# Attention block on one core: the second addition of each VectorE row, the weighted copies of V and the normalising products move to POOL

## The chip, the cores and the metric

The kernel runs on one core of a Trainium2 chip. The metric is the device time of one execution in microseconds, and times of several runs are given as their median. A core has five engines that run side by side, each through its own queue in a fixed order: PE (TensorE, matrix products), ACT (ScalarE), DVE (VectorE), POOL (GpSimd) and SP (SyncE, here only DMAs). They wait for one another through semaphores. An instruction that waits holds up everything behind it on its engine.

## The reference

```python
B, S, D = x.shape            # 1, 2048, 448
H = 16; Dh = D // H          # 28
qkv = (x @ wqkv).reshape(B, S, 3, H, Dh).transpose(2, 0, 3, 1, 4)
q, k, v = qkv[0], qkv[1], qkv[2]
scores = einsum("bhqd,bhkd->bhqk", q, k) * (Dh ** -0.5)
p = softmax(scores, axis=-1)
o = einsum("bhqk,bhkd->bhqd", p, v)
return o.transpose(0, 2, 1, 3).reshape(B, S, D) @ wo
```

All tensors are bf16. It is a whole attention block without a mask: three projections, 16 heads of width 28 over 2048 positions, and an output projection.

## The kernel before, in words

The work is cut into 16 units: four groups of four heads, g, times four chunks of 512 queries, c. Unit u has 16 steps over the keys, 128 keys each. One step of one unit is called a row here, and 256 rows are numbered r = 16u + kt. A row is four tiles, one for each head of the group: 128 keys by 512 queries of scores. So there are 1024 tiles.

PE writes the scores of a tile into one bank of PSUM (s_mm, line 904). The exponential is then made in one of two ways.

- Most tiles go to ACT. It reads three or two banks at once (banks 0 to 2 and 3 to 4 in turn) and writes bf16 exponentials into PT (line 966). PE then multiplies PT with V in one pass of four products (line 871).
- The rows in PLAN["rows"], 67 of them before, go to DVE. It reads each of the four tiles from one of the three other banks (pool "M") and writes the sum of score and constant, cut off below, as int16 into DY (line 928, called D1 here). These bits, read as fp16, are a rough exponential. To make it finer, two shifted copies of the whole row, DS0 and DS1, are made from DY by adding a constant to 128x2048 int16 values (line 936). PE makes three passes for such a row: DY with V, and DS0 and DS1 with two weighted copies of V, called VW (line 859; 32 of them over the kernel, 128x512 each). DY and DS have three buffers each (NDR, NDS), so at most three rows of this kind are under way.

A bank of pool "M" is also held through each unit by the sums that the passes build up, and the rest serve D1's tiles, the projections, the output projection and zero products that PE runs as filling (line 484).

After a unit DVE copies the sums to OTS (line 723). For units 0 to 13 four DMAs on SP's queue (L1 to L4, with a reciprocal on DVE at line 733) bring the reciprocals of the row sums, spread over partitions, into RB, and DVE multiplies RB with OTS (line 739, called NM). Units 14 and 15 do this through PE (norm_pe, last_unit). With the last group of heads the output projection follows (line 710), its result is copied to OUTS by DVE (line 698) and stored by a DMA (line 700). For the last unit ACT makes two of the four copies (line 696), and ACT's own queue issues their DMAs.

The order on every engine is not written by hand. Each instruction is put down with P.add, with its dependencies, a duration in ns and a priority, and schedule() (line 125) lays the instructions out on a timetable made of these durations; each engine then runs its list in that order. The durations are thus part of the order and no more than that: on the chip only dependencies and the order count. CFG holds weights of this planner, PLAN the rows for DVE and the due times of later projections. CFG["dlead"] says how many tiles ahead of its own place a DVE row may start (line 978), and nslack how long after the planned landing of its DMA the NM is placed.

Of the kernel before, what the change touches and what calls it, by code (L numbers as in the profile page):

```python
# [7 lines left out]
ALU = mybir.AluOpType  # L8
# [55 lines left out]
class _Prog:  # L64
# [272 lines left out]
PHASE = (0, 344, 682)  # L337
# [3 lines left out]
ZLO = -ZADD  # L341


CFG = {"late": 4.5, "load": 1.5, "load0": 18, "dcost": 2.3, "dlead": 30.385592406, "aslack": 235.147215477, "opp": 0.0, "oload": 2.5, "klead": 0.405674492, "vlag": 0.024622608, "hot1": 45000.0, "hotm": 3600.0, "nslack": 2585.717981114, "dlook": 20.0, "plook": 471.074451806, "rcost": 4.9, "rlead": 1.0, "rend": 4, "rgap": 2, "acost": 0.4455, "dprio": 0.651412491, "nride": 4, "rslack": 300.0, "stail": 24, "jprio": -0.750113813, "sdlap": 4.771128299, "vwlead": 1.249363626, "sdpen": 6.528606395, "rcostx": -0.000676632}

PLAN = {
    "rows": [9, 14, 16, 24, 26, 28, 33, 38, 41, 50, 53, 54, 57, 61, 62, 70, 72, 77, 80, 84, 88, 95, 97, 98, 103, 107, 109, 111, 113, 117, 123, 125, 131, 135, 138, 139, 141, 148, 149, 152, 162, 163, 164, 165, 169, 176, 177, 179, 180, 187, 189, 190, 193, 199, 200, 207, 211, 212, 213, 215, 222, 229, 231, 234, 235, 244, 248],
    "late": [1.281070854, 1.964014751, 1.915657661, 0.76, 2.743900482, 1.159356603, 1.904466413, 1.845975994, 2.106524837, 2.189415295, 2.428349574, 2.873971098, 2.728623137, 3.84085501, 2.733578841, 4.131340808, 3.508351422, 5.446684044, 4.832243098, 4.46548081, 5.163206443, 7.002171665, 6.90767575, 7.804407036, 4.947925744, 6.78739139, 5.302922841, 6.89552453, 9.777227448, 10.389677342, 7.735503962, 7.490566717, 8.23514301, 7.360578973, 7.83742904, 10.319692841, 8.329224918, 8.680463746],
}


def _fast(nc, x, wqkv, wo, out, n_heads=16):
# [9 lines left out]
    NK = NST  # L362
    QCH = 512
    NCH = S // QCH
    NQT = QCH // 128
# [3 lines left out]
    NDR = 3  # L369
    NDS = 3  # L370
    NPH = len(PHASE)
    NMENG = "dve"
    NOB = 4
    scale = float(DH) ** -0.5
    VONE = DH
# [5 lines left out]
    of = out.rearrange("b s d -> (b s) d")  # L381
# [4 lines left out]
    P = _Prog()  # L386
    es = ExitStack()
    with es:
# [66 lines left out]
        def dma_of(t, g):  # L455
# [3 lines left out]
                      dur=300, prio=-12, name="iota")  # L459
        id_f_op = P.add("dve", lambda e: e.tensor_scalar(id_f[:, :], iota_i[:, :], 0.0, None, ALU.is_equal),  # L460
                        deps=[io_op], dur=250, prio=-10, name="id_f")
# [6 lines left out]
        def zero_pass(acc_open, t):  # L468
# [12 lines left out]
            def emit(e):  # L481
                ins = None
                for h in range(4):
# [13 lines left out]
                       deps=[id_f_op], dur=100, prio=-6, name="sel")  # L497
# [194 lines left out]
        def out_tile(n, opm, hold, eng, pr):  # L692
            oi = outs_n[0] % NOB
            outs_n[0] += 1
            if eng == "act":
                fe = (lambda e: e.activation(OUTS[:, oi, :], bank(hold.banks[0])[:, 0:D], AF.Identity))  # L696
            else:
                fe = (lambda e: e.tensor_copy(OUTS[:, oi, :], bank(hold.banks[0])[:, 0:D]))  # L698
            opev = P.add(eng, fe, deps=[opm, outs_last[oi]], dur=550, prio=pr, name=f"OPEV{n}", rel=[(hold, 0)])
            outs_last[oi] = P.add("act" if eng == "act" else "sp", (lambda e: e.dma_start(of[n * 128:(n + 1) * 128, :], OUTS[:, oi, :])),  # L700
                                  deps=[opev], after=[outs_last[oi]], dur=60, prio=pr, name=f"ODMA{n}", dma_group=grp_out[oi],
                                  nbytes=128 * D * 2)

# [15 lines left out]
        def post_unit(u, last_pv):  # L719
            g, c = units[u]  # L720
            ub = u % 2
            pr = u + 1.02
            accev = P.add("dve", (lambda e: e.tensor_copy(OTS[:, ub, :], bank(pv_open[u].banks[0]))),  # L723
                          deps=[last_pv, ots_last[ub]], dur=610, prio=pr - 60.0, name=f"ACCEV{u}", rel=[(pv_open[u], 0)])
            us = slice(u * 16, (u + 1) * 16)
            if u == NU - 2:
                norm_pe(u, accev, pr)
                return
            l1 = P.add("sp", (lambda e: e.dma_start(scr_l[u], OTS[VONE:128:32, ub, :])), deps=[accev], dur=100, prio=pr,
                       name=f"L1_{u}", dma_group=grp_l[0], nbytes=8192)  # L730
# [8 lines left out]
            nm = P.add(NMENG, (lambda e: e.tensor_tensor(OTN[:, g, c * QCH:(c + 1) * QCH], RB[:, ub, :], OTS[:, ub, :], ALU.mult)),  # L739
                       deps=[l4] + list(xt_ev.values()), dur=1200 if NMENG == "pool" else 610, prio=pr + 0.2, name=f"NM{u}", slack=CFG["nslack"])  # L740
            ots_last[ub] = nm
            finish_unit(g, c, nm, pr)

# [98 lines left out]
        def pv(u, kt):  # L842
# [13 lines left out]

            if r in n_row and (g, kt // 4) not in vw_ev:
                c4 = kt // 4
                vw_ev[(g, c4)] = [P.add("dve", (lambda e, k=k: e.tensor_scalar(VW[:, g % 2, k, 4 * c4:4 * c4 + 4, :], V[:, 4 * c4:4 * c4 + 4, g * 128:(g + 1) * 128],
                                                                              WTERM[k + 1], None, ALU.mult)),  # L860
                                        deps=[v_ev[(g, c4)], vw_used.get((g % 2, c4))], dur=200, prio=u + kt / NK - CFG["vwlead"], name=f"VW{k}_{g}_{c4}")
                                  for k in range(NPH - 1)]

            def weights(k, h):
# [46 lines left out]
        def row_tile(r, h, partner, p_pr):  # L911
            u, kt = r // NK, r % NK
            g, c = units[u]
            t = (u, kt, h)
            if r not in n_row:
                n_row[r] = len(n_row)
                row_ops[r] = []
            ri = n_row[r] % NDR
            old = row_pv.get((n_row[r] - NDR, 0))
            prev_row = row_at.get(n_row[r] - NDR, [])  # L920
            assert n_row[r] < NDR or old is not None, "DVE rows too close"
            deps = [kq_ev[(0, g, c)], kq_ev[(1, g, kt // 4)]]
# [5 lines left out]
            o1 = P.add("dve", (lambda e, ri=ri, h=h, s=s: e.tensor_scalar(DY[:, ri, h * 512:(h + 1) * 512], bank(s.banks[0]), ZLO, ZADD, ALU.max, ALU.add)),  # L928
                       deps=[s, old] + prev_row, dur=600, prio=-90.0, name=f"D1_{r}_{h}", rel=[(s, 0)])
# [6 lines left out]
            row_ev[r] = [P.add("dve", (lambda e, k=k: e.tensor_scalar(DS[:, k, rk, :], DY[:, ri, :], float(PHASE[k + 1]), None, ALU.add)),  # L936
                               deps=row_ops[r] + [row_pv.get((n_row[r] - NDS, k + 1))], dur=600, prio=pr + 0.001 * k, name=f"DS{k}_{r}") for k in range(NPH - 1)]
            row_at[n_row[r]] = row_ev[r]
            done.update(4 * r + j for j in range(4))

# [811 lines left out]
```

## Time and profile before

| | |
|---|---|
| median of 3 runs | 362.06 us (362.02 to 362.64) |
| the profiled execution | 362.26 us |
| its span, first to last instruction | 360.4 us |
| PE, ACT, DVE, POOL busy | 342.2, 345.5, 321.8, 3.4 us |
| granted TensorE clock | 1.000 |
| DMA traffic | 9.91 MB |

Busy time is the union of an engine's instructions; where instructions overlap in the records, the sum of their durations is larger. PE's products are pipelined and partly run beside one another, so that a busy PE isn't a PE at its peak. The view of instruction groups gives source line, engine, operation, output and input with shape, the count, then the busy time in us and the mean of one in ns, and then the idle time of the engine just before these instructions and what ended it. The timeline gives start and length in us.

### The profile page before, as it was taken

How to read it: one execution, taken by the hardware profiler on the slowest of the kernel's cores; microseconds unless marked ns; L12 is line 12 of the kernel's file. 1: busy time of each engine (PE TensorE's matmuls, PEld its weight loads, DVE VectorE, ACT ScalarE, POOL GpSimd, SP SyncE). 2: the span in 40 equal slices, each digit the busy share in tenths (PEclk: the TensorE clock that was granted, in tenths of full speed). 3: DMA queues.
4: the chain of work that ended last, by engine and by line, in shares of the span. 5: the costliest groups of instructions: out<-in, count | busy, mean ns of one | idle time of the engine just before them, and what ended most of it. 6: DMA issues, size and time to landing. Idle time of an engine off the chain costs nothing.

```text
span 360.4 us, 8848 instructions
## 1 busy us (share of the span) xinstructions
PE 342.2 (95%) x3885; PEld 114.4 (32%) x3885; DVE 321.8 (89%) x574; ACT 345.5 (96%) x307; POOL 3.4 (1%) x9
## 2 busy tenths in 40 slices
PE   8999999999999999999999999999998989999996
PEld 4444322332223243223333323332222222234323
DVE  6579999798999999999999998999999999999504
ACT  2999999999999999999999999999999999999992
POOL 3000000000000000000000000000000000000000
PEclk9999999999999999999999999999999999999999
DMA  8600000100100000000000000000000001010201
GB/s 232 152 2 3 2 32 5 32 2 3 33 0 5 32 18 17 2 32 3 20 15 5 31 2 32 3 14 22 29 4 3 20 15 32 16 44 28 78 29 54
DMA packets 13940, 9.91 MB, mean 27 GB/s; under 512 B 7504, under 2 KB 12048, under 8 KB 13896
## 3 DMA queue, kind: packets, MB, share of 16 engines
q1 hardware_dynamic: 13096, 8.74, 8.4%
q8 instruction: 31, 0.51, 0.6%
q10 hardware_dynamic: 800, 0.56, 0.5%
q14 instruction: 13, 0.11, 0.1%
HBM read 7.23 MB, written 2.06 MB: 26 GB/s over the span
## 4 chain that ended last, share of the span: by engine, by line
ACT 88%; PE 11%; issue 0%; ACTq 0%; DVE 0%
ACT PT L966 87%; PE ps L904 3%; PE ps L871 2%; PE ps L555 2%; PE ps L484 1%; PE ps L789 1%; PE ps L572 0%; PE ps L538 0%; ACT OUTS L696 0%; PE ps L824 0%; PE ps L758 0%; PE ps L809 0%; PE ps L769 0%; PE ps L710 0%; ACT QT L524 0%
## 5 line engine op out<-in xcount | busy, mean ns | idle before, releaser
L966 ACT ACTIVATE PT<-ps 128x1536 bf16<-128x1536 f32 (+1 forms) x303 | 342.5, 1398 | 1.0 <-PE ps L904 0.9
L928 DVE TENSOR_SCALAR DY<-ps 128x512 int16<-128x512 f32 x268 | 175.4, 685 | 9.3 <-PE ps L904 8.1
L904 PE MATMUL ps<-QT,KT 28*128 28x512 bf16 x1024 | 151.6, 384 | 12.9 <-ACT PT L966 8.4
L936 DVE TENSOR_SCALAR DS<-DY 128x2048 int16<-128x2048 int16 x134 | 89.9, 683 | 0.4
L904 PEld LDWEIGHTS ps<-QT,KT 28*128 28x128 bf16 x1024 | 39.7, 91 | 139.0 <-ACT PT L966 101.5
L871 PE MATMUL ps<-PT,V 128*32 128x512 bf16 x756 | 65.8, 385 | 0.7 <-DVE OTS L723 0.4
L871 PE MATMUL ps<-DS,VW 128*32 128x512 f16 x536 | 49.3, 385 | 0.1
L555 PE MATMUL ps<-xT,w_raw 112*32 112x512 bf16 x512 | 35.8, 381 | 0.0
L484 PE MATMUL ps<-ZM,ZW 128*32 128x512 bf16 x324 | 29.5, 410 | 1.2 <-DVE ZM L466 1.2
L871 PE MATMUL ps<-DY,V 128*32 128x512 f16 x268 | 26.5, 385 | 0.1
L871 PEld LDWEIGHTS ps<-PT,V 128*32 128x32 bf16 x756 | 17.1, 94 | 28.4 <-issue 21.9
L871 PEld LDWEIGHTS ps<-DS,VW 128*32 128x32 bf16 x536 | 12.5, 94 | 20.5 <-issue 13.7
L572 PE MATMUL ps<-w_raw,xT 112*128 112x112 bf16 x256 | 17.1, 214 | 0.0
L555 PEld LDWEIGHTS ps<-xT,w_raw 112*32 112x32 bf16 x512 | 12.2, 95 | 13.1 <-issue 3.8
L698 DVE CAST OUTS<-ps 128x448 bf16<-128x448 f32 x14 | 8.6, 622 | 7.6 <-PE ps L710 7.2
L572 PEld LDWEIGHTS ps<-w_raw,xT 112*128 112x128 bf16 x256 | 13.0, 98 | 6.7 <-issue 4.7
L528 DVE CAST KT<-ps 128x512 bf16<-128x512 f32 x16 | 11.0, 689 | 3.5 <-PE ps L555 3.4
L484 PEld LDWEIGHTS ps<-ZM,ZW 128*32 128x32 bf16 x324 | 7.8, 99 | 13.6 <-issue 10.9
L528 DVE CAST V<-ps 128x448 bf16<-128x448 f32 x16 | 9.9, 621 | 2.0 <-PE ps L572 1.9
L526 DVE TENSOR_SCALAR QT<-ps 128x512 bf16<-128x512 f32 x15 | 10.3, 686 | 1.5 <-PE ps L555 1.5
L710 PE MATMUL ps<-wop,XO 128*128 128x448 bf16 x48 | 11.5, 355 | 0.0
L723 DVE COPY OTS<-ps 128x512 f32<-128x512 f32 x15 | 10.3, 687 | 0.5 <-PE ps L871 0.5
(49 smaller groups left out, 79.2 us busy)
## 6 DMA issues: line engine op xcount, KB each, us to landing
RB<-scr_r SPq DMA_DIRECT2D x14, 256.0 KB
out_dram<-OUTS SPq DMA_DIRECT2D x14, 112.0 KB, 1.7
XO<-in_x_dram SPq DMA_DIRECT2D x3, 448.0 KB, 6.3
w_raw<-in_wqkv_dram SPq DMA_DIRECT2D x5, 196.0 KB, 6.3
wop<-in_wo_dram SPq DMA_DIRECT2D x16, 24.5 KB
XO<-in_x_dram SPq DMA_DIRECT2D x1, 224.0 KB, 3.5
XO<-in_x_dram ACTq DMA_DIRECT2D x1, 224.0 KB, 4.0
scr_l<-OTS SPq DMA_DIRECT2D x14, 8.0 KB
```

Source lines behind the costliest of these rows:

```text
L484: ins = e.matmul(ps[32 * h:32 * h + 32, b * 512:(b + 1) * 512], ZW[:, :], ZM[:, :], start=shut, stop=shut, skip_group_check=not shut, tile ...
L526: fe = (lambda e: e.tensor_scalar(evac[0](), evac[1](hold[0].banks[0]), mul, None, ALU.mult))
L528: fe = (lambda e: e.tensor_copy(evac[0](), evac[1](hold[0].banks[0])))
L555: ins = e.matmul(ps[32 * h:32 * h + 32, b * 512:(b + 1) * 512], w_raw[0:IT, it, col:col + 32], xT[0:IT, it, c * 512:(c + 1) * 512], start= ...
L572: ins = e.matmul(ps[:, b * 512 + j * GD:b * 512 + (j + 1) * GD], xT[0:IT, it, n * 128:(n + 1) * 128], w_raw[0:IT, it, 2 * D + g * GD:2 * D ...
L710: return e.matmul(bank(hold[0].banks[0])[:, 0:D], OTN[:, gg, n * 128:(n + 1) * 128], wop[:, gg, :], start=(gg == 0), stop=(gg == G - 1))
L723: accev = P.add("dve", (lambda e: e.tensor_copy(OTS[:, ub, :], bank(pv_open[u].banks[0]))), deps=[last_pv, ots_last[ub]], dur=610, prio=pr ...
L871: ins = e.matmul(ps[32 * h:32 * h + 32, b * 512:(b + 1) * 512], weights(k, h), p_[h], start=(kt == 0 and k == 0), stop=(kt == NK - 1 and k ...
L904: ins = e.matmul(bank(b), KT[32 * h:32 * h + rows, g, kt * 128:(kt + 1) * 128], QT[32 * h:32 * h + rows, g, c * QCH:(c + 1) * QCH], start= ...
L928: o1 = P.add("dve", (lambda e, ri=ri, h=h, s=s: e.tensor_scalar(DY[:, ri, h * 512:(h + 1) * 512], bank(s.banks[0]), ZLO, ZADD, ALU.max, AL ...
L936: row_ev[r] = [P.add("dve", (lambda e, k=k: e.tensor_scalar(DS[:, k, rk, :], DY[:, ri, :], float(PHASE[k + 1]), None, ALU.add)), deps=row_ ...
L966: ex = P.add("act", (lambda e, p0=p0, w=w, bf=bf: e.activation(PT[:, p0 * 512:(p0 + w) * 512], bank(bf(), w), AF.Exp, scale=ESCALE)), deps ...
```

## The change

- DS0 stays on DVE and DS1 goes to POOL. In the planner they now count 740 and 2900 ns, both 600 before.
- All VW copies go to POOL (790 ns in the planner instead of 200).
- NM of units 0 to 13 goes to POOL (NMENG; 1400 ns in the planner, 610 on DVE).
- In the last unit only one of ACT's two output DMAs stays in ACT's queue, the other goes to SP's.
- PLAN["rows"] has 69 rows in place of 67, and PLAN["late"] and several weights in CFG have new values, among them dlead (30.39 becomes 49.00) and nslack (2586 becomes 2004). So the order on each engine is another one throughout.

```diff
-    "rows": [9, 14, 16, 24, 26, 28, 33, 38, 41, 50, ..., 229, 231, 234, 235, 244, 248],
+    "rows": [9, 14, 16, 23, 27, 30, 35, 37, 39, 52, ..., 227, 232, 234, 235, 242, 253],
...
-    NMENG = "dve"
+    NMENG = "pool"
...
-            outs_last[oi] = P.add("act" if eng == "act" else "sp", (lambda e: e.dma_start(of[n * 128:(n + 1) * 128, :], OUTS[:, oi, :])),
+            outs_last[oi] = P.add("act" if eng == "act" and n % NQT == 2 else "sp", (lambda e: e.dma_start(of[n * 128:(n + 1) * 128, :], OUTS[:, oi, :])),
...
-                       deps=[l4] + list(xt_ev.values()), dur=1200 if NMENG == "pool" else 610, prio=pr + 0.2, name=f"NM{u}", slack=CFG["nslack"])
+                       deps=[l4] + list(xt_ev.values()), dur=1400 if NMENG == "pool" else 610, prio=pr + 0.2, name=f"NM{u}", slack=CFG["nslack"])
...
-                vw_ev[(g, c4)] = [P.add("dve", (lambda e, k=k: e.tensor_scalar(VW[:, g % 2, k, 4 * c4:4 * c4 + 4, :], V[:, 4 * c4:4 * c4 + 4, g * 128:(g + 1) * 128],
+                vw_ev[(g, c4)] = [P.add("pool", (lambda e, k=k: e.tensor_scalar(VW[:, g % 2, k, 4 * c4:4 * c4 + 4, :], V[:, 4 * c4:4 * c4 + 4, g * 128:(g + 1) * 128],
                                                                               WTERM[k + 1], None, ALU.mult)),
-                                        deps=[v_ev[(g, c4)], vw_used.get((g % 2, c4))], dur=200, prio=u + kt / NK - CFG["vwlead"], name=f"VW{k}_{g}_{c4}")
+                                        deps=[v_ev[(g, c4)], vw_used.get((g % 2, c4))], dur=790, prio=u + kt / NK - CFG["vwlead"], name=f"VW{k}_{g}_{c4}")
...
-            row_ev[r] = [P.add("dve", (lambda e, k=k: e.tensor_scalar(DS[:, k, rk, :], DY[:, ri, :], float(PHASE[k + 1]), None, ALU.add)),
-                               deps=row_ops[r] + [row_pv.get((n_row[r] - NDS, k + 1))], dur=600, prio=pr + 0.001 * k, name=f"DS{k}_{r}") for k in range(NPH - 1)]
+            row_ev[r] = [P.add(("dve", "pool")[k], (lambda e, k=k: e.tensor_scalar(DS[:, k, rk, :], DY[:, ri, :], float(PHASE[k + 1]), None, ALU.add)),
+                               deps=row_ops[r] + [row_pv.get((n_row[r] - NDS, k + 1))], dur=(740, 2900)[k], prio=pr + 0.001 * k, name=f"DS{k}_{r}") for k in range(NPH - 1)]
```

More of the change, by code (lines that the diff above doesn't have):

```diff
@@ L341 @@
 ZLO = -ZADD
-CFG = {"late": 4.5, "load": 1.5, "load0": 18, "dcost": 2.3, "dlead": 30.385592406, "aslack": 235.147215477, "opp": 0.0, "oload": 2.5, "klead": 0.405674492, "vlag": 0.024622608, "hot1": 45000.0, "hotm": 3600.0, "nslack": 2585.717981114, "dlook": 20.0, "plook": 471.074451806, "rcost": 4.9, "rlead": 1.0, "rend": 4, "rgap": 2, "acost": 0.4455, "dprio": 0.651412491, "nride": 4, "rslack": 300.0, "stail": 24, "jprio": -0.750113813, "sdlap": 4.771128299, "vwlead": 1.249363626, "sdpen": 6.528606395, "rcostx": -0.000676632}
+CFG = {"late": 4.5, "load": 1.5, "load0": 18, "dcost": 2.3, "dlead": 49.004334305, "aslack": 234.737849947, "opp": 0.0, "oload": 2.5, "klead": 0.357086809, "vlag": 0.031136205, "hot1": 45000.0, "hotm": 3600.0, "nslack": 2003.516744081, "dlook": 20.0, "plook": 471.336819277, "rcost": 4.9, "rlead": 1.0, "rend": 4, "rgap": 2, "acost": 0.4455, "dprio": 0.598694735, "nride": 4, "rslack": 300.0, "stail": 24, "jprio": -1.241545043, "sdlap": 1.739709505, "vwlead": 0.239355705, "sdpen": 9.625222564, "rcostx": -0.000676632}
@@ L346 @@
 PLAN = {
-    "rows": [9, 14, 16, 24, 26, 28, 33, 38, 41, 50, 53, 54, 57, 61, 62, 70, 72, 77, 80, 84, 88, 95, 97, 98, 103, 107, 109, 111, 113, 117, 123, 125, 131, 135, 138, 139, 141, 148, 149, 152, 162, 163, 164, 165, 169, 176, 177, 179, 180, 187, 189, 190, 193, 199, 200, 207, 211, 212, 213, 215, 222, 229, 231, 234, 235, 244, 248],
-    "late": [1.281070854, 1.964014751, 1.915657661, 0.76, 2.743900482, 1.159356603, 1.904466413, 1.845975994, 2.106524837, 2.189415295, 2.428349574, 2.873971098, 2.728623137, 3.84085501, 2.733578841, 4.131340808, 3.508351422, 5.446684044, 4.832243098, 4.46548081, 5.163206443, 7.002171665, 6.90767575, 7.804407036, 4.947925744, 6.78739139, 5.302922841, 6.89552453, 9.777227448, 10.389677342, 7.735503962, 7.490566717, 8.23514301, 7.360578973, 7.83742904, 10.319692841, 8.329224918, 8.680463746],
+    "rows": [9, 14, 16, 23, 27, 30, 35, 37, 39, 52, 53, 54, 60, 61, 62, 63, 70, 73, 79, 82, 84, 91, 95, 97, 98, 101, 105, 108, 110, 113, 114, 119, 128, 133, 135, 137, 139, 144, 145, 150, 153, 157, 165, 167, 169, 171, 177, 178, 181, 184, 186, 187, 191, 193, 199, 200, 205, 208, 215, 216, 217, 220, 223, 227, 232, 234, 235, 242, 253],
@@ L349 @@
+    "late": [1.452202241, 2.420047794, 1.210950018, 0.76, 3.157520381, 1.969320385, 1.82825018, 1.56833372, 2.575677089, 2.422590438, 2.120497526, 2.924097519, 2.7973984, 3.842970868, 2.630182944, 4.427234048, 4.389501202, 5.149364556, 5.039227115, 4.355838455, 4.545624487, 6.938179159, 6.628994567, 6.772028123, 4.742746785, 6.417907847, 5.573786372, 5.627627587, 9.767523112, 11.38174923, 7.786274561, 6.798841714, 7.527465064, 7.29630783, 8.234814647, 10.023262478, 9.946790858, 8.457705463],
 }
```

## The prediction

> **What bounds the kernel now.** I read the page first: busy times and the chain that ended last.
>
> ```profile
> span 360.4 us, 8848 instructions
> ...
> PE 342.2 (95%) x3885; PEld 114.4 (32%) x3885; DVE 321.8 (89%) x574; ACT 345.5 (96%) x307; POOL 3.4 (1%) x9
> ...
> ACT 88%; PE 11%; issue 0%; ACTq 0%; DVE 0%
> ```
>
> Three engines are nearly full, so shares alone don't decide. The chain does: 88% of it is ACT. The waits and two stretches of the span confirm it.
>
> ```profile
> PEld ps L904 <- ACT PT L966: 101.5, 268, 0.9
> PEld ps L871 <- DVE DS L936: 4.3, 17, 0.4
> ACT PT L966 <- PE ps L904: 0.9, 2, 0.5
> ```
>
> ```profile
> core 0: us, PE busy (x) PEld busy (x) DVE busy (x) ACT busy (x) POOL busy (x), PEclk, DMA share, GB/s
> 20.00:340.00 320.00, 307.04 (x3499) 99.34 (x3499) 305.10 (x536) 319.47 (x283) 0.00 (x0) 1.00 0.06 17
> 240.00:280.00 40.00, 36.92 (x409) 10.42 (x405) 39.96 (x68) 40.00 (x37) 0.00 (x0) 1.00 0.05 16
> ```
>
> PE came to the scores 268 times before ACT had freed their banks, and waited 101.5 us in all, 0.38 us each time; ACT waited for PE only 0.9 us. From 240 to 280 us DVE had no gap at all (39.96 of 40), yet ACT worked on: DVE is nearly full but holds up nobody. So the time goes by the number of tiles on ACT, as long as what DVE (and now POOL) delivers is late by less than PE's 0.38 us.
>
> **The change part by part.** These rows carry the costs.
>
> ```profile
> L966 ACT ACTIVATE PT<-ps 128x1536 bf16<-128x1536 f32 (+1 forms) x303 | 342.5, 1398 | 1.0 <-PE ps L904 0.9
> ```
>
> ```profile
> L966 ACT ACTIVATE PT<-ps 128x1536 bf16<-128x1536 f32 x151 | 243.2, 1611 | 1.0 <-PE ps L904 0.9
> L966 ACT ACTIVATE PT<-ps 128x1024 bf16<-128x1024 f32 x151 | 179.6, 1189 | 0.0
> L966 ACT ACTIVATE PT<-ps 128x512 bf16<-128x512 f32 x1 | 0.7, 728 | 0.0
> L928 DVE TENSOR_SCALAR DY<-ps 128x512 int16<-128x512 f32 x268 | 175.4, 685 | 9.3 <-PE ps L904 8.1
> L936 DVE TENSOR_SCALAR DS<-DY 128x2048 int16<-128x2048 int16 x134 | 89.9, 683 | 0.4
> L871 PE MATMUL ps<-DS,VW 128*32 128x512 f16 x536 | 49.3, 385 | 0.1
> L859 DVE TENSOR_SCALAR VW<-V 128x512 bf16<-128x512 bf16 x32 | 8.2, 287 | 0.2
> L739 DVE TENSOR_TENSOR XO<-RB,OTS 128x512 bf16<-128x512 f32 x14 | 9.6, 684 | 0.0
> L493 POOL MEMSET V<- 128x256 bf16 x1 | 1.2, 1237 | 0.1
> L494 POOL MEMSET wop<- 128x896 int32 x1 | 1.2, 1164 | 0.0
> L492 POOL MEMSET V<- 128x1024 bf16 x1 | 1.0, 951 | 0.0
> ```
>
> *Two more rows on DVE.* ACT makes 151x3 + 151x2 + 1 = 756 tiles in 342.5 us, 0.453 us a tile. Sixty-nine rows leave 1024 - 276 = 748 tiles, eight fewer: -3.6 us. All of it is on the path, since ACT hardly ever waits. For PE the rows add two passes of four products each, 16 products of 49.3/536 = 0.092 us: 1.5 us, behind the 101.5 us in which PE waits for ACT.
>
> *DVE.* It loses 67 additions of 89.9/134 = 0.67 us (45.0 us), all VW (8.2) and 14 NM (9.6): 62.8 us. The two rows bring 8 D1 of 175.4/268 = 0.65 us and 2 DS0 of 0.67: 6.6 us. So 321.8 becomes 265.6 us. From 20 to 340 us DVE had 320 - 305.1 = 14.9 us of gaps, so its room is 321.8 + 14.9 = 336.7 us, 333.1 with the span 3.6 us shorter. What is free is 67.5 us, or 0.98 us a row. In itself this relief is worth nothing, as DVE isn't on the path; it is what the two rows, and any stall of DVE, are paid from.
>
> *POOL.* Before, it did no arithmetic, so its prices are bounded by its memsets: 0.93 ns an element for dense bf16 (951/1024), 1.30 for int32 (1164/896), 4.83 for a strided one (1237/256). For 2048 elements that is 1.9, 2.7 and 9.9 us. DS1 is dense, so the upper of the two dense rows is nearest; a memset reads nothing and an addition does, so I take 2.9 us, the figure for which the order is laid out. For VW and NM the same rows give 512 x 1.30 = 0.67 us, and twice that with two inputs; I take the order's 0.79 and 1.4. POOL's work is 69x2.9 + 32x0.79 + 14x1.4 = 245 us, within 333. [...]
>
> *Waits that are new.* DS1 now waits in POOL's queue behind VW and NM, and NM waits for the DMA that fills RB. If that lands late, the DS1 behind it are late, and PE's third pass, and with it the scores behind that in PE's queue. DS1 comes at least 2.9 - 0.67 = 2.2 us later than on DVE. The larger lead covers this: a row may start 49 tiles ahead instead of 30, at 0.453 us a tile up to 22 instead of 14 us (three buffers permitting). NM holds OTS 0.7 us longer, and a unit lasts 360.4/16 = 22 us. Bounds: a gain of at most the 0.9 us that ACT waited before, and a loss of 3.4 us (rival B). I take a loss of 0.3, near the row of ACT's waits.
>
> *The port.* The first microseconds show POOL and DVE side by side.
>
> ```profile
> 1.00 0.95 POOL L492 MEMSET V<- 128x1024 bf16 x1
> 1.09 0.94 DVE L460 TENSOR_SCALAR id_f<-iota_i 128x128 f32<-128x128 int32 x1
> 2.01 1.24 POOL L493 MEMSET V<- 128x256 bf16 x1
> 2.06 2.01 DVE L462 CAST id_b<-id_f 128x128 bf16<-128x128 f32 x1
> 2.83 1.16 POOL L494 MEMSET wop<- 128x896 int32 x1
> ```
>
> DVE's cast of 128 elements takes 2.01 us, where VW takes 0.29 us for 512. It starts 0.05 us after a memset and ends at 4.07, just after the second one (3.99); the TENSOR_SCALAR above it ends at 2.03, after POOL's 1.95. So DVE work from SBUF to SBUF stands still while POOL works. DS0 is such an instruction, DS1 would be POOL's, and both become ready with the same last D1. If DS0 goes first, POOL loses 0.7 us, which is free. If DS1 goes first, DVE stands for up to 2.9 us, with the D1s behind DS0 and their banks. [...]
>
> ```profile
> 149.63 0.68 DVE L928 TENSOR_SCALAR DY<-ps 128x512 int16<-128x512 f32 x1
> 150.34 0.69 DVE L936 TENSOR_SCALAR DS<-DY 128x2048 int16<-128x2048 int16 x1
> ...
> 156.57 1.97 DVE L928 TENSOR_SCALAR DY<-ps 128x512 int16<-128x512 f32 x3
> 158.97 0.69 DVE L928 TENSOR_SCALAR DY<-ps 128x512 int16<-128x512 f32 x1 [0.43 <-PE ps L904]
> 159.58 0.68 DVE L936 TENSOR_SCALAR DS<-DY 128x2048 int16<-128x2048 int16 x1
> ```
>
> Both cases occur in the order before. At 150.34 the addition follows its last D1 by 0.03 us and would win. At 159.58 it stands behind D1s of the next row: counted in fours, its own last D1 is the second of the three at 156.57, ended about 157.8, and a POOL addition begun then would hold it until 160.7. DVE with a sixth less work has a shorter queue, so the first case should become the usual one. I put the mean stall at 0.4 us a row, 28 us of the 67.5: no cost.
>
> *The end.*
>
> ```profile
> 356.42 0.54 ACT L696 ACTIVATE OUTS<-ps 128x448 bf16<-128x448 f32 x1 [3.97 <-PE ps L834]
> 356.60 0.54 PE L834 MATMUL ps<-wop,XO 128*128 128x448 bf16 x2
> 356.61 1.19 DVE L698 CAST OUTS<-ps 128x448 bf16<-128x448 f32 x2 [0.41 <-PE ps L834]
> 357.00 0.38 ACTq L700 DMA_DIRECT2D out_dram<-OUTS  x1
> 357.26 0.90 SPq L700 DMA_DIRECT2D out_dram<-OUTS  x2
> 357.47 0.54 ACT L696 ACTIVATE OUTS<-ps 128x448 bf16<-128x448 f32 x1 [0.51 <-PE ps L1007]
> 358.05 0.35 ACTq L700 DMA_DIRECT2D out_dram<-OUTS  x1
> ```
>
> ACT issues its first output DMA from 357.00 to 357.38 and only then makes its second copy, although the product for it was done by 357.14 (356.60 + 0.54). With that DMA on SP's queue ACT's last issue ends about 0.3 us sooner than 358.40; then SP's last, at 357.26 + 0.90 = 358.16 and now behind one more DMA, is late next. I take -0.2, between 0 and -0.3.
>
> *The sum,* against the profiled execution: span 360.4 - 3.6 - 0.2 + 0.3 = 356.9 us, and 1.86 us around it (362.26 - 360.4): 358.8. The median of the runs is 0.2 below the profiled one: 358.6 us.
>
> **The rivals.** *B, the gain is eaten on the way:* DS1 comes late for PE's third pass, by the 0.7 us for which DS0 may hold the port, which the order doesn't know. PE's slack is 0.38 us, so 0.3 us passes to ACT each time. Before, 17 of 134 additions were waited for; if a sixth of the 69 are, 11 x 0.3 = 3.4 us, and the time is about 362.0. For it: the timetable knows no port. Against it: the larger lead.
>
> *C, DVE stalls at the port and becomes the bound (slower).* A DS0 that stands behind one D1 (0.6 us) when DS1 starts waits 2.9 - 0.6 = 2.3 us. It decides from 0.98 us a row, that is when 43% of rows go so. At half of them: 265.6 + 69x1.15 = 345 us against 333, 12 us over, about 370.6 us; at three quarters, 385 us, 52 over, about 410. [...] For it: in the order before most additions stood behind something, as at 159.58. Against it: that queue came from a DVE without gaps; and while DVE stands, POOL finishes, so the next pair meets an empty port.
>
> *D, POOL becomes the bound:* from (333 - 45)/69 = 4.2 us a DS1 on; at the strided memset's 9.9 us POOL alone has 728 us of work. The dense rows speak against it. To it belongs that POOL might hold D1 too: by turns, 265.6 + 245 = 511 us of work. No row shows D1 beside POOL. [...]
>
> **How the numbers follow.** A, the forecast, 0.60, with a range of its own from 357.4 to 360.4; B 0.13; C 0.24; D 0.03. No change means within 0.2% (361.3 to 362.8), about what runs from 362.02 to 362.64 can tell. B splits: 0.04 faster, 0.07 same, 0.02 slower. So faster 0.64, same 0.07, slower 0.29. The low end, 357.4, is A with the whole 0.3 us at the end, no new waits and 0.7 of ACT's 1.0 us of idling gone; I leave 0.05 below it. Upwards the range takes in B and the nearer half of C, to 370; half of C and D, 0.15, lie above.
>
> **What the profile after would show.** Right: L966 in 300 instructions with about 339 us busy and 1 to 2 us of waiting before them; ACT's share of the chain unchanged; DVE's busy time, stalls included, at 270 to 310 us; DS0 at 0.7 us in most rows, some 2 to 3; L936 on POOL near 2.9 us. C would show as DS0 with a mean over 1.7 us and long waits of PE for D1; B as PE's waits for POOL's DS of 0.5 us and more, and ACT's idle time at 3 to 5 us; D as POOL without gaps. D1 clearly above 0.685 us would make the whole account of DVE wrong.

## The result: half as long again, and the profile after

The changed kernel takes 558.23 us (553.89 to 559.60, 4 runs) against 362.12 us before: ratio 1.539, interval 1.531 to 1.548. The profiled execution took 558.6 us. Executions that took over 1.5% longer than the fastest one of their kernel are left out of all medians, ranges and ratios below, and a kernel of which one execution is left has no ratio. The page of the changed kernel, with its rows for ACT and POOL, the granted clock and the chain:

```profile
span 556.5 us, 8905 instructions
...
PE 450.0 (81%) x3849; PEld 119.8 (22%) x3849; DVE 432.8 (78%) x471; ACT 356.9 (64%) x304; POOL 461.9 (83%) x124
...
ACT  4994656876477656693856656756544455567685
POOL 2699958797699999899998999998875876799940
PEclk9996575867567766795877756975556566558799
...
PE 32%; POOL 30%; DVE 19%; issue 12%; ACT 6%; DMA 1%; SPq 0%; POOLq 0%
```

ACT, 88% of the chain before, is 6% of it now; PE, POOL and DVE alternate on it. No engine is full, and the TensorE clock, 1.000 before, is granted at 0.709. The groups of instructions of the changed kernel show where POOL's 462 us come from:

```profile
L966 ACT ACTIVATE PT<-ps 128x1536 bf16<-128x1536 f32 (+1 forms) x300 | 353.9, 1263 | 186.2 <-PE ps L904 181.0
L936 POOL TENSOR_SCALAR DS<-DY 128x2048 int16<-128x2048 int16 x69 | 388.4, 5640 | 58.1 <-DVE DY L928 56.3
L928 DVE TENSOR_SCALAR DY<-ps 128x512 int16<-128x512 f32 x276 | 181.6, 682 | 73.0 <-PE ps L904 70.7
L936 DVE TENSOR_SCALAR DS<-DY 128x2048 int16<-128x2048 int16 x69 | 196.9, 2854 | 1.1
L859 POOL TENSOR_SCALAR VW<-V 128x512 bf16<-128x512 bf16 x32 | 49.9, 1560 | 17.7 <-DVE V L528 15.6
L739 POOL TENSOR_TENSOR XO<-RB,OTS 128x512 bf16<-128x512 f32 x14 | 21.1, 1510 | 0.0
```

DS1 takes 5.64 us, not 2.9; VW 1.56, not 0.79. DS0, 0.68 us of work on DVE, lasts 2.85 us on average. D1 still takes 0.68 us. The waits of the changed kernel (total us, times, longest):

```profile
ACT PT L966 <- PE ps L904: 181.0, 115, 7.2
...
DVE DY L928 <- PE ps L904: 70.7, 82, 7.1
PEld ps L904 <- DVE DY L928: 67.6, 78, 3.8
POOL DS L936 <- DVE DY L928: 56.3, 25, 5.6
...
PEld ps L871 <- POOL DS L936: 42.4, 21, 7.6
...
PEld ps L871 <- DVE DS L936: 26.5, 10, 4.1
```

Before, PE waited for ACT and ACT for nobody. Now PE waits up to 7.6 us for DS1, and 67.6 us in all (15.7 before) until a late D1 frees a bank for its scores; ACT waits 181 us for PE's scores. The timeline shows the first such stop:

```profile
39.30 6.70 POOL L859 TENSOR_SCALAR VW<-V 128x512 bf16<-128x512 bf16 x4
...
43.89 0.39 PE L871 MATMUL ps<-DS,VW 128*32 128x512 f16 x4
...
45.97 10.69 POOL L936 TENSOR_SCALAR DS<-DY 128x2048 int16<-128x2048 int16 x2
...
51.39 0.62 PE L871 MATMUL ps<-DS,VW 128*32 128x512 f16 x4 [7.11 <-POOL DS L936]
...
52.59 2.53 ACT L966 ACTIVATE PT<-ps 128x1536 bf16<-128x1536 f32 x2 [7.21 <-PE ps L904]
52.63 0.69 DVE L928 TENSOR_SCALAR DY<-ps 128x512 int16<-128x512 f32 x1 [7.09 <-PE ps L904]
```

Four VW hold POOL for 6.70 us, where the order counts 3.2. DS1 starts at 45.97, PE's third pass waits 7.11 us for it, and behind that pass, in PE's queue, stand the scores for ACT and for D1: all three engines stop. A pass of four products, 0.39 us before the stop, takes 0.62 us after it, with the clock at 0.50 (46 to 70 us). Two longer stretches of the span of the changed kernel:

```profile
core 0: us, PE busy (x) PEld busy (x) DVE busy (x) ACT busy (x) POOL busy (x), PEclk, DMA share, GB/s
...
20.00:40.00 20.00, 19.46 (x218) 7.62 (x215) 13.85 (x23) 20.00 (x19) 18.44 (x7) 1.00 0.01 2
40.00:100.00 60.00, 48.53 (x387) 11.62 (x387) 35.70 (x44) 36.83 (x31) 52.29 (x16) 0.60 0.04 11
```

Up to 40 us ACT is full, as forecast; from 40 to 100 us the clock is 0.60 and ACT works 36.8 of 60 us. DS0 beside DS1, later in the timeline of the changed kernel:

```profile
142.54 5.36 POOL L936 TENSOR_SCALAR DS<-DY 128x2048 int16<-128x2048 int16 x1 [2.61 <-DVE DY L928]
142.98 5.48 DVE L936 TENSOR_SCALAR DS<-DY 128x2048 int16<-128x2048 int16 x1
```

POOL starts 0.44 us sooner and ends at 147.90; DVE ends at 148.46, 0.56 us later. In 47 of the 69 rows DS0 lasted over 1.0 us, and each of these ended 0.54 to 0.56 us after a DS1 that had begun before it. "The port" is in this document a name for this standstill; the runs show its times, not what the two engines share.

**Theories.** T1: POOL's true price, and DVE's stalls at the port, make POOL and DVE the bound; PE's stops and the lower clock follow from it. T2: the order is laid out for prices that don't hold; PE stops by turns for late data, runs at half clock after each stop, and with a right order most of the loss would go. T3: the new order or the other moves (VW, NM, the rows) cost time even at the assumed prices.

### The profile page after: what moved, and what is told of

Same layout as the page of the kernel before. It is cut to its first block, busy times and chain, and to the rows that moved or that the text cites. A ratio compares the mean times of both kernels' runs of the same rounds, so it can differ in the third digit from the quotient of the medians.

```text
span 556.5 us, 8905 instructions
## 1 busy us (share of the span) xinstructions
PE 450.0 (81%) x3849; PEld 119.8 (22%) x3849; DVE 432.8 (78%) x471; ACT 356.9 (64%) x304; POOL 461.9 (83%) x124
## 4 chain that ended last, share of the span: by engine, by line
PE 32%; POOL 30%; DVE 19%; issue 12%; ACT 6%; DMA 1%; SPq 0%; POOLq 0%
POOL DS L936 24%; DVE DS L936 14%; PE ps L904 13%; PE ps L871 12%; ACT PT L966 6%; DVE DY L928 4%; POOL VW L859 4%; PE ps L555 4%; PE ps L484 2%; POOL XO L739 2%; DMA XO<-in_x_dram 1%; PE ps L572 1%; PE ps L538 0%; PE ps L789 0%; PE ps L769 0%
## 5 line engine op out<-in xcount | busy, mean ns | idle before, releaser
L966 ACT ACTIVATE PT<-ps 128x1536 bf16<-128x1536 f32 (+1 forms) x300 | 353.9, 1263 | 186.2 <-PE ps L904 181.0
L936 POOL TENSOR_SCALAR DS<-DY 128x2048 int16<-128x2048 int16 x69 | 388.4, 5640 | 58.1 <-DVE DY L928 56.3
L904 PE MATMUL ps<-QT,KT 28*128 28x512 bf16 x1024 | 191.8, 499 | 34.5 <-DVE DY L928 28.4
L936 DVE TENSOR_SCALAR DS<-DY 128x2048 int16<-128x2048 int16 x69 | 196.9, 2854 | 1.1
L871 PE MATMUL ps<-DS,VW 128*32 128x512 f16 x552 | 69.0, 507 | 54.0 <-POOL DS L936 32.4
L871 PE MATMUL ps<-PT,V 128*32 128x512 bf16 x748 | 88.5, 522 | 5.8 <-DVE DY L928 3.0
L859 POOL TENSOR_SCALAR VW<-V 128x512 bf16<-128x512 bf16 x32 | 49.9, 1560 | 17.7 <-DVE V L528 15.6
L555 PE MATMUL ps<-xT,w_raw 112*32 112x512 bf16 x512 | 49.3, 498 | 2.1 <-DVE DY L928 2.1
L871 PE MATMUL ps<-DY,V 128*32 128x512 f16 x276 | 36.6, 521 | 0.6 <-DVE DY L928 0.4
L739 POOL TENSOR_TENSOR XO<-RB,OTS 128x512 bf16<-128x512 f32 x14 | 21.1, 1510 | 0.0
L555 PEld LDWEIGHTS ps<-xT,w_raw 112*32 112x32 bf16 x512 | 14.4, 113 | 23.5 <-issue 18.7
```

Of the source, the lines that this page charges most:

```text
L555: ins = e.matmul(ps[32 * h:32 * h + 32, b * 512:(b + 1) * 512], w_raw[0:IT, it, col:col + 32], xT[0:IT, it, c * 512:(c + 1) * 512], start= ...
L859: vw_ev[(g, c4)] = [P.add("pool", (lambda e, k=k: e.tensor_scalar(VW[:, g % 2, k, 4 * c4:4 * c4 + 4, :], V[:, 4 * c4:4 * c4 + 4, g * 128:( ...
L871: ins = e.matmul(ps[32 * h:32 * h + 32, b * 512:(b + 1) * 512], weights(k, h), p_[h], start=(kt == 0 and k == 0), stop=(kt == NK - 1 and k ...
L904: ins = e.matmul(bank(b), KT[32 * h:32 * h + rows, g, kt * 128:(kt + 1) * 128], QT[32 * h:32 * h + rows, g, c * QCH:(c + 1) * QCH], start= ...
L936: row_ev[r] = [P.add(("dve", "pool")[k], (lambda e, k=k: e.tensor_scalar(DS[:, k, rk, :], DY[:, ri, :], float(PHASE[k + 1]), None, ALU.add ...
L966: ex = P.add("act", (lambda e, p0=p0, w=w, bf=bf: e.activation(PT[:, p0 * 512:(p0 + w) * 512], bank(bf(), w), AF.Exp, scale=ESCALE)), deps ...
```

## The experiments

The first one measures prices by themselves; the others change the kernel. Unless said otherwise, they keep the changed kernel's order on every engine. Line numbers are up to four higher where the edit adds lines.

**1. Prices by themselves.** A kernel of its own, with nothing of the attention in it: POOL instructions alone, beside PSUM reads on DVE, and beside additions on DVE.

> A kernel that computes nothing of the attention block: it only runs POOL's additions by themselves and beside DVE, and writes zeros. Price theory (POOL's addition of 128x2048 int16 is slow by itself, the 5.64 us of the changed kernel being its own price): 5.2 to 5.6 us alone, about the same beside DVE instructions that read PSUM. Port theory (it costs about 2.9 us alone, and DVE's work doubles it): 2.7 to 3.1 us alone, over 5 us only beside DVE additions. For the copies of V (128x512 bf16) 1.5 us against 0.8 us. An integer addition of 128x1024 int32 with the same bytes: 2.5 to 3.1 us under the price theory, as it has half the elements.

Its timeline:

```profile
12.18 16.26 POOL L49 TENSOR_SCALAR B<-A 128x2048 int16<-128x2048 int16 x3 [11.76 <-DVE ps L48]
28.52 1.49 POOL L52 TENSOR_SCALAR B<-A 128x512 int16<-128x512 int16 x1
30.09 2.77 POOL L53 TENSOR_SCALAR B<-A 128x1024 int16<-128x1024 int16 x1
...
39.97 5.37 POOL L56 TENSOR_SCALAR BF<-AF 128x2048 f32<-128x2048 f32 x1
45.42 1.89 POOL L57 TENSOR_TENSOR BI<-AI,C 128x1024 int32<-128x1024 int32 x1
...
49.41 19.54 DVE L64 TENSOR_SCALAR G<-ps 128x512 int16<-128x512 f32 x27
49.46 16.27 POOL L49 TENSOR_SCALAR B<-A 128x2048 int16<-128x2048 int16 x3 [0.81 <-DVE G L62]
...
69.83 5.37 POOL L49 TENSOR_SCALAR B<-A 128x2048 int16<-128x2048 int16 x1 [4.10 <-DVE G L70]
71.24 4.51 DVE L73 TENSOR_SCALAR E<-D 128x2048 int16<-128x2048 int16 x1
```

With one input POOL takes 1.49, 2.77 and 5.37 us for 512, 1024 and 2048 elements: 2.5 ns an element ((5.37 - 2.77)/1024) and 0.2 us, the same for int16, bf16 and f32. The 5.37 us are what the price theory expected (5.2 to 5.6). Reads of PSUM on DVE, D1's kind, leave POOL at 16.27 for three and themselves at 0.69 each. An addition on DVE that starts 1.41 us after POOL's ends at 75.75, 0.55 us after POOL's 75.20. So here the addition from SBUF to SBUF waits for the whole of POOL's (4.51 us), and the one that reads PSUM doesn't (0.69).

**2 and 3. One addition left out.** In the one kernel pass 3 reads DS0 in place of DS1, in the other pass 2 reads DY in place of DS0. Their orders are new, since the planner has fewer instructions.

```diff
+# no_ds1
+terms = [DY[:, ri, :], DS[:, 0, rk, :], DS[:, 0, rk, :]]
+# no_ds0
+terms = [DY[:, ri, :], DY[:, ri, :], DS[:, 1, rk, :]]
```

> The changed kernel without the second addition: PE's third pass reads the first addition's result in its place. All else is as changed: 69 rows, VW and NM on POOL, the end. Price theory: with about 71 us of POOL work left, nothing is late, and the time is the forecast 358.6 us, within 1 us. Port theory: DVE's first addition can still meet VW and NM (46 instructions of 1.5 us), so some of the loss stays: 362 to 370 us. If the new order itself were at fault: over 400 us.

371.31 us, ratio 1.024 (1.021 to 1.027), just above what the port theory expected. Nearly all of the loss goes with DS1, which speaks for T1 and T2. The remaining 9 us can't be read: the new order has 388 zero products instead of 272.

> The changed kernel without the first addition: PE's second pass reads DY, and DVE runs no addition from SBUF to SBUF any more; POOL still makes the second one. Price theory: POOL's work stays at 69x5.4 + 32x1.55 + 14x1.5 = 443 us, so the time stays at 490 to 550 us. Port theory: without DVE at the port POOL's addition falls towards 2.9 us and the time to about 360 us.

501.73 us in one execution, at a clock of 0.77. DS1 took 5.36 us and POOL was busy for 436.7 us. POOL's price alone makes most of the loss; the meeting with DS0 adds to it.

**4. A cheaper DS1:** the same sums, two int16 values at a time as int32.

```diff
+CST = sb("CST", [128, 1], I32)   # filled with PHASE[2] * 65537
-e.tensor_scalar(DS[:, k, rk, :], DY[:, ri, :], float(PHASE[k + 1]), None, ALU.add)
+e.tensor_tensor(i32v(DS[:, 1, rk, :]), i32v(DY[:, ri, :]), CST[:, :].to_broadcast([128, 1024]), ALU.add)
```

> The changed kernel with the second addition made on the same bytes as 128x1024 int32 (adding 682 to both halves at once), so that POOL has half the elements; order laid for 2.9 us as before. Price theory: POOL's addition takes about 2.8 us, which is what the forecast assumed, so the time is near the forecast: 358 to 364 us. Port theory: POOL's addition still meets DVE's and the time stays above 400 us.

385.46 us, ratio 1.066 (1.063 to 1.069), between the two expectations. DS1 has a median of 1.89 us, less than the order counts, yet the kernel is slower than before: VW takes 1.54 us, DS0 1.21 us on average, and ACT waits 23.5 us. So a cheap DS1 takes back 173 us of the loss and doesn't bring the forecast gain.

**5 to 8. Price and port apart, in the same order.** DS1 works on 32 or 1024 of its columns, or on all; DS0 stays, or becomes a memset of 600 columns on DVE, which reads nothing from SBUF.

```diff
+fe0 = (lambda e: e.memset(DS[:, 0, rk, 0:600], PHASE[1]))   # *_noport
+fe1 = (lambda e: e.tensor_scalar(DS[:, 1, rk, 0:1024], DY[:, ri, 0:1024], float(PHASE[2]), None, ALU.add))   # 0:32, 0:2048
```

> The changed kernel with every instruction in the order as changed, but POOL's second addition covers only 32 of the 2048 columns (the others keep zeros from one memset at the start), so that it costs about 0.3 us. It asks whether the new order by itself gives the forecast. If POOL's addition, by price or port, is the whole cause: 358 to 360 us. If the order with 69 rows, or VW and NM on POOL, costs something by itself: 363 us or more, as without the second addition (371.3 us, but there the planner laid a new order).

> The same with 1024 of the 2048 columns in POOL's second addition: 2.8 us alone, nearly the 2.9 us that the prediction took. Pure price theory: the forecast holds, 358 to 362 us. Port theory: VectorE's first addition stands behind POOL's, 1 us and more on average, D1 comes late and ScalarE starves: 385 to 420 us, above the 386 us of the integer form, which takes 1.9 us alone.

> As before with 1024 columns, and VectorE's first addition replaced by a memset of 600 columns that takes about 0.7 us too and reads nothing from SBUF (the addition's result is left out). Port theory: the memset doesn't meet POOL, VectorE no longer stands, 358 to 366 us. If the lateness of POOL's result (not the port) holds PE: no gain against the run with the addition.

> The changed kernel with POOL's second addition whole (5.4 us alone) and VectorE's first addition replaced by the memset of 600 columns. It splits the loss of the changed kernel at full price: price theory says 480 to 510 us (POOL's 440 us of work and what waits for it), so the port's own part is about 50 us of 196; port theory says below 420 us.

| DS1 | its time, us | DS0 | median, us (range) |
|---|---|---|---|
| 32 columns | 0.54 | addition | 366.26 (364.82 to 370.27) |
| 1024 columns | 2.99 | addition | 377.00 (one execution) |
| 1024 columns | 2.77 | memset, 0.56 us | 365.50 (365.22 to 365.79) |
| whole | 5.36 | memset, 0.56 us | 484.23 (one execution) |
| whole (the change) | 5.64 | addition | 558.23 |

For the first row the ratio is 1.009 (1.007 to 1.011): with next to no DS1 this order is still not faster than the kernel before. The second row lies between its two expectations. Between the third and fourth rows only POOL's price differs: +118.7 us. Between the fourth and fifth DS0 becomes the addition again, and meets POOL's: +74.0 us. At 2.77 us for DS1, the forecast's price within 5%, and without the port, the ratio is 1.009 (1.007 to 1.011): still no gain. The timeline and two stretches of this third kernel show where ACT loses time (columns as above):

```profile
206.07 0.40 PE L872 MATMUL ps<-DY,V 128*32 128x512 f16 x4 [1.71 <-issue]
...
209.71 0.62 PE L872 MATMUL ps<-DS,VW 128*32 128x512 f16 x4
```

```profile
203.00:206.00 3.00, 1.36 (x24) 0.90 (x20) 1.78 (x3) 2.85 (x3) 3.00 (x2) 1.00 0.09 31
...
209.00:212.00 3.00, 2.83 (x21) 0.77 (x25) 0.69 (x1) 2.19 (x2) 2.92 (x3) 0.50 0.02 5
```

PE stops once, for 1.71 us, released by nothing that the profile shows, at a product at which its program takes a jump. From 208.9 to 215.8 us the clock is 0.50. ACT waits 7.2 us for PE over the whole kernel, 4.5 of them between 205 and 214 us. The only stop before that is the one of 1.71 us, with PE busy for 1.36 of 3.00 us.

**9 and 10. The jump.** PE's jump goes to the end of its program, once without and once with the port.

```diff
-P.JUMP_AT = {"pe": "PV8_11", "dve": f"OPEV{n0 - 1}", "act": f"OPEV{n0}", "sp": "L1_0"}
+P.JUMP_AT = {"dve": f"OPEV{n0 - 1}", "act": f"OPEV{n0}", "sp": "L1_0"}
```

> The run with 1024 columns and the memset in place of VectorE's first addition, and PE's jump to the second part of its program moved from the product PV8_11 (near 205 us) to the end of PE's work. In the runs so far PE stands 1.5 to 1.7 us at just that product with nothing to wait for, and its clock is at half for some 6 us behind it. Jump theory: without the jump there both go, and the time is the forecast's, 358 to 360 us, as POOL's price is the assumed one and the port is free. If the stop at 205 us has another cause: 365.5 us as before.

> The run with 1024 columns and VectorE's first addition in place, with PE's jump at the end as well. It prices the port alone, at the 2.8 us for POOL's addition that the prediction assumed, against the run without the addition: port theory 370 to 378 us; if the port costs nothing at this price: the same as the run without the addition, 358 to 360 us.

Without the port 368.50 us, ratio 1.016 (1.010 to 1.021), against 365.50: no gain. With it 374.45 us, 1.030 (1.023 to 1.038), against 377.00. So the jump as the cause of the lost gain falls. In the first of them the stop at 204 to 206 us is gone, but its timeline has a new one a little later:

```profile
209.69 6.08 POOL L860 TENSOR_SCALAR VW<-V 128x512 bf16<-128x512 bf16 x4
...
215.73 8.24 POOL L938 TENSOR_SCALAR DS<-DY 128x1024 int16<-128x1024 int16 x3
...
218.56 0.62 PE L872 MATMUL ps<-DS,VW 128*32 128x512 f16 x4 [2.90 <-POOL DS L938]
```

Four VW hold POOL for 6.08 us, DS1 comes late by them, PE stops for 2.90 us, and the clock is 0.50 from 216.9 to 230.6 us.

**11 and 12. VW at its assumed price too.** It works on 256 of 512 columns (0.85 us; the order counts 0.79), first without the port, then with it.

```diff
-e.tensor_scalar(VW[:, g % 2, k, 4 * c4:4 * c4 + 4, :], V[:, 4 * c4:4 * c4 + 4, g * 128:(g + 1) * 128],
+e.tensor_scalar(VW[:, g % 2, k, 4 * c4:4 * c4 + 2, :], V[:, 4 * c4:4 * c4 + 2, g * 128:(g + 1) * 128],
```

> The run without the port and with PE's jump at the end, and the copies of V on POOL cut to 256 of 512 columns (about 0.85 us each, near the 0.79 us that the order assumes; the others keep zeros). Now every price on POOL is the one that the prediction took, and VectorE can't meet POOL at the port. If wrong prices and the port are all that failed, no stop of PE is left and the time is the forecast's: 357.5 to 360 us. If a stop of PE of 1.5 us or more with half the clock behind it remains, some other wait is at work and the time stays at 365 to 369 us.

> The same with VectorE's first addition in place of the memset: the world of the prediction, all POOL prices as assumed, and the port as it is. The prediction's forecast case says 358 to 360 us (stalls of 0.4 us a row are paid from VectorE's gaps). Port theory: stops of VectorE pass to PE now and then and set off the half clock: 365 to 376 us.

Without the port 360.40 us (359.91 to 360.96), ratio 0.995 (0.994 to 0.997). This is the forecast's world, and in it half of the gain is there: 1.8 us where 3.5 were forecast. The group of ACT's exponentials and the chain of this kernel:

```profile
L970 ACT ACTIVATE PT<-ps 128x1536 bf16<-128x1536 f32 (+1 forms) x300 | 338.7, 1395 | 2.2 <-PE ps L906 2.2
```

```profile
ACT 91%; PE 5%; DMA 2%; SPq 0%; issue 0%; DVE 0%
```

With the port 363.65 us (363.26 to 367.37), ratio 1.005 (1.002 to 1.009), between the two expectations: the gain is gone. The groups of this kernel, in an execution of 365.31 us:

```profile
L938 DVE TENSOR_SCALAR DS<-DY 128x2048 int16<-128x2048 int16 x69 | 61.8, 896 | 1.1
...
L970 ACT ACTIVATE PT<-ps 128x1536 bf16<-128x1536 f32 (+1 forms) x300 | 340.3, 1342 | 6.1 <-PE ps L906 5.6
```

The 3.2 us are too little for a DS1 of 2.9 us, though. In the timeline of the kernel with 1024 columns (run 6) DVE gets through before POOL is done; in that of the int32 addition (run 4) it doesn't:

```profile
112.41 2.77 POOL L938 TENSOR_SCALAR DS<-DY 128x1024 int16<-128x1024 int16 x1 [0.69 <-DVE DY L929]
112.85 1.15 DVE L937 TENSOR_SCALAR DS<-DY 128x2048 int16<-128x2048 int16 x1
```

```profile
100.43 1.89 POOL L940 TENSOR_TENSOR DS<-DY,CST 128x1024 int32<-128x1024 int32 x1 [2.53 <-PE ps L873]
100.87 2.01 DVE L938 TENSOR_SCALAR DS<-DY 128x2048 int16<-128x2048 int16 x1
```

In run 6 DVE ends at 114.00, 1.18 us ahead of POOL's 115.18; no DS0 in that run lasts over 1.53 us. In run 4 it ends at 102.88, after POOL's 102.32; 23 of 69 last over 1.8 us. So the cut DS1 holds DVE for less than its length, other than the whole one in experiment 1. This fits the slower int32 kernel, although its DS1 is shorter; why the cut one lets DVE through isn't known.

**13. The order laid out for the true prices.** This tells T1 from T2; PE's jump is at the end, and rows and weights are as in the change.

```diff
-dur=(740, 2900)[k]   ...   dur=790 (VW)    ...   dur=1400 (NM)
+dur=(1000, 5700)[k]  ...   dur=1550 (VW)   ...   dur=1300 (NM)
```

> The changed kernel with its work unchanged, but the order laid anew with the prices that were measured: 5700 ns for POOL's addition, 1000 for VectorE's, 1550 for a copy of V, 1300 for a normalising product (and PE's jump at its end). Capacity theory (POOL's work, 69x5.4 + 32x1.5 + 14x1.3 = 439 us, sets the time whatever the order): 485 to 510 us, with the clock at 0.95 or more, since the order then fills PE's waits with zero products. If the wrong prices in the order cost little: 540 to 560 us as before, with the clock near 0.7.

541.18 us in one execution. Two groups of this kernel:

```profile
L936 POOL TENSOR_SCALAR DS<-DY 128x2048 int16<-128x2048 int16 x69 | 389.4, 5662 | 19.5 <-DVE DY L928 19.5
...
L484 PE MATMUL ps<-ZM,ZW 128*32 128x512 bf16 x2008 | 156.9, 404 | 1.2 <-DVE ZM L466 1.2
```

PE is filled with 2008 zero products in place of 272, and the clock is 0.933 instead of 0.709; that takes back 17 us of 196. The time is thus what the second expectation said, the clock nearly what the first did. T2 falls as the main cause: POOL's work stays, 463.2 us here and some 436 even at the prices it has alone (69 x 5.37 + 32 x 1.49 + 14 x 1.26), and DVE's DS0 lasts 2.41 us on average. An order searched anew for these prices wasn't tried.

**14 and 15. The other moves alone.** 69 rows; both additions on DVE again, VW and NM on POOL at 1560 and 1300 ns; then NM alone on POOL. Rows, due times and weights were searched anew with the planner, and PE's jump is at the end.

```diff
-row_ev[r] = [P.add(("dve", "pool")[k], ..., dur=(740, 2900)[k], ...
+row_ev[r] = [P.add("dve", ..., dur=600, ...
```

> The changed kernel with the second addition back on VectorE; the copies of V (1.5 us each) and the normalising products stay on POOL; 69 rows, an order found anew for these prices, and PE's jump at its end. If POOL's second addition alone is at fault, and the 46 remaining POOL instructions seldom meet VectorE's 138 additions: 358.5 to 360.5 us, faster than the kernel before. Port theory: VectorE has hardly any gaps here, and a meeting costs it up to 1.5 us, so some stops reach PE: 361 to 368 us.

> Only the normalising products of units 0 to 13 on POOL (14 of 1.3 us); both additions and the copies of V on VectorE; 69 rows, an order of its own, and PE's jump at its end. With 14 short POOL instructions the port hardly matters: 359.5 to 361.5 us, a little faster than the kernel before. If VectorE with 99% of its time taken can't carry 69 rows: 362 us or more.

The first takes 362.24 us (360.52 to 363.82, 12 runs), ratio 0.999 (0.997 to 1.001): no change, and within the port theory's range. VW on POOL and two rows more bring nothing here: ACT does 300 instructions, but its waits come to 3.7 us and the clock to 0.995. The second takes 365.63 us, ratio 1.009 (1.006 to 1.012), with DVE busy for 327.3 us; that is the second expectation. T3 accounts for a few us, not for the loss. No kernel that does the whole computation was faster than the one before.

## Why the prediction was wrong, step by step

**The step that failed is DS1's price on POOL:** "DS1 is dense, so the upper of the two dense rows is nearest; a memset reads nothing and an addition does, so I take 2.9 us". It took 5.37 us alone and 5.64 in the kernel. A memset only writes, and so was no upper bound for an instruction that reads, computes and writes; of the three rows only the strided one, 9.9 us, was. VW went the same way (0.79 taken, 1.56 measured), NM less so (1.4 and 1.51). POOL's work, 245 us in the sum, is 69 x 5.64 + 32 x 1.56 + 14 x 1.51 = 460 us, and 333 were to be had. That is rival D, with its bound of 4.2 us a DS1 and a chance of 0.03. Its sign, POOL without gaps, isn't there: POOL still waited 56.3 us for the D1 of a DVE that stands.

**The second is the port,** "I put the mean stall at 0.4 us a row". It was 2.85 - 0.68 = 2.17 us a row, beyond the 0.98 from which rival C decides, and DS0 lasted over 1.0 us in 47 of 69 rows (68%), where C needed 43%. C's sign, long waits of PE for D1, is there: 67.6 us. The prediction paired DS0 with the DS1 of its own row alone, and expected a shorter queue on DVE to let DS0 go first. In the main that came true: both engines take the rows in ascending order, and counted so DS0 starts ahead of its own row's DS1 in 52 of 69 rows. But POOL was behind. In 31 of the 47 rows with such a long DS0 it met the DS1 of an earlier row, as here in the timeline of the changed kernel:

```profile
258.34 11.55 POOL L936 TENSOR_SCALAR DS<-DY 128x2048 int16<-128x2048 int16 x2
...
260.13 4.54 DVE L936 TENSOR_SCALAR DS<-DY 128x2048 int16<-128x2048 int16 x1
```

This DS0 follows its own last D1 at once (260.10 us). The first of POOL's two DS1, until about 264.1, is that of the row before, and DS0 stands until it ends. In the other 16 it met its own row's DS1, as in the pair shown for the changed kernel: from 140.40 to 143.06 us DVE makes four D1 in a row, POOL's DS1 starts at 142.54, within the fourth, which thus belongs to another row, and DS0 comes after it at 142.98. That is rival C's case of one D1 in between. Each kind makes up about half of the stalled time. So C and D came true together, and half of C by way of D: a DS1 of twice the price leaves POOL with a backlog, and DS0 meets it. In run 13, too, DS0 starts ahead of its own DS1 in 67 of 69 rows, and 44 of its 49 long ones met an earlier row's. That DVE stands while POOL works was right (DS0 of up to 5.70 us); the price put on it reckoned with pairs of one row. A DS0 that goes first holds POOL too, for less than the prediction's 0.7 us: in the changed kernel the 41 DS1 that start while a DS0 runs take 5.79 to 5.87 us, and 27 of the other 28 take 5.36 or 5.37. The last, at 24.25 us, takes 6.07, and there the DS0 that starts 0.16 us after it takes only 0.68.

Even at a small price "no cost" was wrong. In run 12, with DS1 near 2.9 us, the mean stall was 0.896 - 0.683 = 0.21 us a row, within the 0.4, and still 3.2 us went against run 11. In four of its six executions the clock was 0.997 or more, at 363.3 to 363.9 us, so these 3 us aren't the clock's. In the profiled one 26 of 69 DS0 lasted over 1.0 us, and PE's longest wait for D1 was 1.1 us where run 11 has 0.5. A stall longer than PE's slack of 0.38 us can reach ACT, whatever gaps DVE has elsewhere: a mean over rows doesn't show that.

**The account.** Along one path of experiments the gap of 199.6 us between forecast and result divides so (run 8 is one execution):

| from, to | us | what changes |
|---|---|---|
| 358.6 to 360.4 | +1.8 | assumed prices, no port: what the sum had wrong (run 11) |
| 360.4 to 365.5 | +5.1 | VW at its true price, jump as in the change (run 7) |
| 365.5 to 484.2 | +118.7 | DS1 at its true price (run 8) |
| 484.2 to 558.2 | +74.0 | DS0 meets DS1 at the port (the change) |

The port's share depends on where it is put: at a DS1 cut to 2.77 us it is 3.2 (run 12 against 11), 5.9 (10 against 9) or 11.5 us (6 against 7).

**A mechanism that the forecast lacked** is what a stop costs behind it. PE's waits for ACT before, of up to 0.9 us, cost ACT nothing. In runs 6, 7, 9 and 10 each of the six stops of 1.5 us or more leaves ACT waiting and is followed by 6.8 to 20.5 us at half clock, in which PE makes too few scores for ACT. Rivals C and D counted the work of one engine. By D's own working run 8 should take 358.6 + 69 x 5.36 + 32 x 1.49 + 14 x 1.27 - 333 = 461 us; it took 484.2. I read the 23 us between as PE's stops and the lower clock; they weren't measured apart. Of the whole loss the lower clock is the smaller part, as far as one execution of another order can tell: in run 13 it rose to 0.933, for 17 us of 196.

**What was right.** *ACT:* 300 instructions, 338.7 us in run 11 where about 339 were forecast, and 91% of the chain. *D1* beside POOL: 682 ns, 685 before. *The end* went wrong by a little: in run 11 the last exponential ends at 349.66 of 358.1 us, and SP's three issues are late next:

```profile
353.63 1.11 ACT L698 ACTIVATE OUTS<-ps 128x448 bf16<-128x448 f32 x2 [3.97 <-PE ps L836]
...
354.20 2.11 SPq L702 DMA_DIRECT2D out_dram<-OUTS  x3
```

They end at 356.31, 6.65 us after the last exponential; before, the last issue ended 5.95 us after it (352.45 to 358.40). So -0.2 was +0.7. With ACT's waits of 2.2 instead of 1.3 us that more than covers the 1.1 us by which this execution, at 359.91 us, exceeds the 358.8 of the sum.

**What stays open:** why PE stops at its jump in this order, when it doesn't in the kernel before; why a DS1 on half the columns frees the port early; what sets the moment at which the clock falls; and what a full DS0 that avoids the port would bring, which wasn't tried.

## What to carry to other kernels

Before work goes to an engine that has done none, measure the very instruction there, with its inputs, type and length: a row of another operation bounds nothing. Then ask what the two engines share, and price the meeting by the order in which they really start, with everything the other engine is still behind with, not by the pair that is hoped for. And where an engine in order feeds several others, count a late input as a stop of all of them, with the half clock that followed here (6.8 to 20.5 us of it after each of the six stops in runs 6, 7, 9 and 10).

## What the runs showed of the hardware

- POOL needed 2.5 ns an element for a TENSOR_SCALAR, int16, bf16 or f32 alike (5.37 us for 2048, experiment 1). The two TENSOR_TENSOR tried were quicker: 1.89 us for 1024 int32 elements (one input a single column) against 2.77 for 1024 int16, and 1.26 against 1.49 us for 512 (f32 in, bf16 out).
- One stop of PE of 1.71 us (run 7) was followed by 6.8 us at half the granted clock, from 2.9 us after it; one of 2.90 us (run 9) by 13.7 us, from within the stop. Run 12 shows the half clock without such a stop: it is 0.50 from 300.8 to 311.0 us, and in the 3.4 us before PE was busy for 2.85, with no stop over 0.55 us.
- A TENSOR_SCALAR of 2048 columns on POOL kept an addition on DVE waiting to its end (5.48 us for 0.68 us of work, the change), an int32 TENSOR_TENSOR too (2.01 us, run 4); one of 1024 int16 columns did so for less than its length (1.15 us, POOL 2.77, run 6). An addition on DVE that ran when POOL's TENSOR_SCALAR of 2048 columns began made that one 5.79 to 5.87 us long, against 5.36 or 5.37 (the change).
